# Attention and gated feed-forward on one core: the first quarter of the program put in a written order on all five engines

## The chip, the cores and the metric

The program runs on one core of a Trainium2 chip. The metric is the time of one execution in device microseconds. The core has five engines, each with its own instruction queue that it works off strictly in order: PE (TensorE: matmuls and transposes), ACT (ScalarE), DVE (VectorE), POOL (GpSimd) and SP (SyncE, which here only issues DMA transfers). Engines wait for each other through semaphores. PE writes only to PSUM, on-chip accumulators; POOL works in SBUF, the other on-chip memory.

## The reference

Four sequences of 768 positions and 8 heads of 64 go through local attention with block summaries. The result, heads side by side, is the input of a feed-forward layer with a convolution gate.

```python
# attention, per batch and head; block = 32, window = 16
k_sum = k.reshape(B, H, nb, block, D).max(axis=3)
v_sum = v.reshape(B, H, nb, block, D).mean(axis=3)
scores_l = where(|i - j| < window, q @ k.T / sqrt(D), -1e9)
scores_s = q @ k_sum.T / sqrt(D) + log(block)
a = softmax(concatenate([scores_l, scores_s]))
x = a @ concatenate([v, v_sum])
# feed-forward, per batch; x is [768, 512], d_ff = 1024
h = relu(x @ w_in)
conv = conv_w[0] * h[s-1] + conv_w[1] * h[s] + conv_w[2] * h[s+1]
out = (h * sigmoid(conv)) @ w_out
```

`w_in`, `conv_w` and `w_out` reach the core as 64-bit floats, so the kernel also turns their words into 32-bit numbers.

## The kernel before

**Tiles.** The rows are cut into 8 *chunks* of 384 (two per batch, c = 0 to 7). In a chunk, attention goes by 4 *pairs* of heads; pairs are numbered through, so pair n belongs to chunk n // 4. The feed-forward part of a chunk goes by 8 *units*, one for each 128 of the 1024 hidden columns.

**A pair.** Keys `kw` (a window of 96 and 24 block maxima for each of 6 query blocks), queries `q` and values `va` come by DMA. `qk` (line 256) is 12 small matmuls that use 64 rows of PE each: six for the first head, six for the second, in turn, into two PSUM tiles `pq_0` and `pq_1`. DVE adds the mask (278), ACT takes exponentials with their sums (288), DVE inverts the sums (296, 297), and DVE in chunk 0 or POOL later multiplies (300). `tr` (308) is three transposes for one head into the PSUM tile `pt`, of which there is one; ACT, or DVE for half of chunk 0, copies it to `aT` (313, 315). `av` (329) is 12 matmuls for the pair. ACT rounds the result to `xh` (349), DVE takes the rest `xl` (350).

**A unit.** `f1` (411): 12 matmuls of 384 columns, three (high by high, low by high, high by low) for each of four pieces of the contraction; piece cc needs only pair cc of the chunk. Then relu (429), three taps (432 or 434, and 441 twice), tanh (458), product (459), and high and low part of the result, `ghi` (462, ACT) and `glo` (463, POOL). `f2` (480) multiplies finished gates with `w_out`, three matmuls of 512 columns for each step.

**Weights.** A block of `w_in` or `w_out` (eight each) is loaded, decoded (ACT 93, DVE 100 and 101), rounded to a high part by ACT (124) and a low part by POOL (125).

**What sets the order.** In chunks 0 and 1 the framework's scheduler orders every engine from the order in which the code issues work (`slot`, `slot_t`, `slot_av`, `unit`). It may place single matmuls of `qk`, `f1` and `av` apart, and adds *warm* matmuls on zeros (line 78). From chunk 2 on, PE runs in the order of the code and the others are scheduled. DMAs of inputs are issued by SP in order; each waits until the one eight places before it has landed.

Of the kernel before, what the change touches and what calls it, by code (L numbers as in the profile page):

```python
# [16 lines left out]
P = 128  # L17
# [23 lines left out]
EARLY_IN = 2  # L41

OUT_AT = (6, 7, 8, 9, 10, 10, 11, 12)
WARM = {"start": 10, "pq0": 5, "pq1": 12, "pq2": 3, "pq3": 3, "tr": 2, "av": 3, "unit": 3}
EARLY_AT = 3
ORDERED = 2
NGROUP = NCHUNK * NP * 2
# [3 lines left out]
def attention_ffn(ctx, tc, qT, kT, vT, v4, w_in, cwT, w_out, mask8, ident_in, out):  # L51
# [23 lines left out]
    def warm(where, after=None):  # L75
        def go():
            for i in range(WARM.get(where, 0)):
                nc.tensor.matmul(pw, idle[:, :P], idle, start=True, stop=True)  # L78

        if after is None:  # L80
            go()
        else:
            with tc.issue_after(after):
                go()

    warm("start")


    def decode(out, words, n, name):
        lo_word = words[:, 0 : 2 * n : 2]  # L90
        hi_word = words[:, 1 : 2 * n : 2]
        low = sp.tile([P, DM], U32, tag="wl", name=f"wl_{name}", bufs=1)[:, :n]
        nc.scalar.activation(  # L93
            out.bitcast(F32),
            hi_word.bitcast(F32),
            AF.Prelu,
            scale=2.0**-112,
            alpha=2.0**32,
        )
        nc.vector.tensor_scalar(low, lo_word, 29, None, ALU.logical_shift_right)  # L100
# [4 lines left out]
    def load_in(fc):  # L105
        t = raw_a[:, fc, :] if fc < 6 else raw_b[:, fc - 6, :]
        nc.sync.dma_start(t, w_in[fc].bitcast(U32))
        return t

    def split_in(fc, t):  # L110
        weights(t, flat(win_hi, fc), flat(win_lo, fc), f"i{fc}")

    def load_out(fc):
        t = sp.tile([P, 1024], U32, tag="stage", name=f"wo{fc}", bufs=2)
        nc.sync.dma_start(t, w_out[fc].bitcast(U32))
        return t
# [80 lines left out]

    def prep_pair(c, p):
        b, hf = divmod(c, 2)
        st = state[(c, p)]  # L200
        kw = st["kw"]
        if hf == 0:
            k = st["k"]
            ks = cp.tile([P, NB], F32, tag=f"ks{p}", name=f"ks{c * NP + p}")
            kv = k[:, WIN:KL].rearrange("p (n t) -> p n t", t=BLK)
            nc.vector.tensor_reduce(ks, kv, AX.X, ALU.max)
            state[("ks", b, p)] = ks
        if c == 0:
            (nc.gpsimd if p else nc.vector).tensor_copy(
                kw[:, :, :WK], window(k, 1, list(k.ap[0]), WK)  # L210
            )
        ks = state[("ks", b, p)]
        nc.gpsimd.tensor_copy(
            kw[:, :, WK:NK], ks.unsqueeze(1).to_broadcast([P, CB, NB])
        )

    def vmean_pair(c, p):

        b, hf = divmod(c, 2)
        if hf:  # L220
# [12 lines left out]
        if c == 0:
            nc.gpsimd.tensor_copy(
                st["va"][WK:NK, :, :], vm.unsqueeze(1).to_broadcast([NB, CB, P])
            )
        state[("vm", b, p)] = vm

    def group(j):
        c, r = divmod(j, NP * 2)  # L240
        p, t = divmod(r, 2)
        return c, p, t

    def qk(c, p):


        st = state[(c, p)]
        n = c * NP + p
        pq = [
            ps.tile([P, 512], F32, tag="s", name=f"pq{n}_{h}", bufs=2) for h in range(2)  # L250
        ]
        for blk in range(CB):
            i, half = divmod(blk, 2)
            for h in range(2):
                r = slice(h * QB, (h + 1) * QB)
                last = nc.tensor.matmul(  # L256
# [6 lines left out]
        if c == 0:  # L263
# [428 lines left out]
```

## Time and profile before

| | us |
|---|---|
| three timed runs | 403.81, 403.69, 402.52 |
| median | 403.69 |
| profiled execution, its own time | 404.54 |
| its span, first to last instruction | 402.7 |
| first matmul of chunk 2's units in it, after the start | 129.1 |

The span is one execution under the profiler. In what follows "us 60" is 60 us after its start. Up to us 129.1 chunks 0 and 1 run; chunks 2 to 7 take the rest. A matmul's row gives its whole passage through the engine, and the next one starts before it ends, so costs on PE are read from start to start.

### The profile page before, as it was taken

How to read it: one execution, taken by the hardware profiler on the slowest of the kernel's cores; microseconds unless marked ns; L12 is line 12 of the kernel's file. 1: busy time of each engine (PE TensorE's matmuls, PEld its weight loads, DVE VectorE, ACT ScalarE, POOL GpSimd, SP SyncE). 2: the span in 40 equal slices, each digit the busy share in tenths (PEclk: the TensorE clock that was granted, in tenths of full speed). 3: DMA queues.
4: the chain of work that ended last, by engine and by line, in shares of the span. 5: the costliest groups of instructions: out<-in, count | busy, mean ns of one | idle time of the engine just before them, and what ended most of it. 6: DMA issues, size and time to landing. Idle time of an engine off the chain costs nothing.

```text
span 402.7 us, 8927 instructions
## 1 busy us (share of the span) xinstructions
PE 389.2 (97%) x3164; PEld 322.0 (80%) x3173; DVE 254.3 (63%) x792; ACT 252.3 (63%) x774; POOL 145.6 (36%) x179
## 2 busy tenths in 40 slices
PE   7989799999799999999999999999999999999996
PEld 3546677787588888888888888888888888999884
DVE  4998767787665775678765566466664655656200
ACT  3665788898776776757565777666665644344211
POOL 2336444575753233332432333323333332222200
PEclk9999699999899999999999999999999999999999
DMA  8999494477887495646233244334210000000011
GB/s 276 315 362 236 110 270 137 131 244 212 248 187 239 134 315 143 186 124 212 55 105 101 79 113 114 112 87 121 70 61 28 28 2 26 27 28 26 28 52 52
DMA packets 45357, 54.30 MB, mean 135 GB/s; under 512 B 24641, under 2 KB 33025, under 8 KB 45313
## 3 DMA queue, kind: packets, MB, share of 16 engines
q1 hardware_dynamic: 41568, 47.19, 40.7%
q10 hardware_dynamic: 3744, 6.54, 4.7%
q8 instruction: 25, 0.41, 0.5%
q14 instruction: 20, 0.16, 0.1%
HBM read 45.36 MB, written 6.29 MB: 128 GB/s over the span
## 4 chain that ended last, share of the span: by engine, by line
PE 86%; DMA 9%; ACT 1%; POOL 1%; issue 1%; SPq 0%; DVE 0%; POOLq 0%; ACTq 0%; DVEq 0%
PE f L411 33%; PE f L480 33%; PE pq L256 7%; PE xp L329 6%; PE pt L308 5%; DMA va<-v 4%; DMA raw_b<-w_in 2%; DMA wo<-w_out 1%; PE pw L78 1%; DMA mask<-mask 1%; DMA q<-qT 1%; ACT wu_i L93 1%; POOL wout_lo L125 0%; POOL win_lo L125 0%; PE pv L230 0%
## 5 line engine op out<-in xcount | busy, mean ns | idle before, releaser
L463 POOL TENSOR_TENSOR glo<-t,ghi 128x383 fp32r<-128x383 f32 (+1 forms) x64 | 65.0, 1015 | 99.2 <-ACT ghi L462 89.3
L411 PE MATMUL f<-xh,win_hi 128*128 128x384 f32 (+1 forms) x256 | 93.9, 367 | 0.1
L288 ACT ACTIVATE a<-a,nm 128x120 f32<-128x120 f32 x192 | 75.0, 392 | 22.7 <-DVE nm L278 18.2
L441 DVE SCALAR_TENSOR_TENSOR t<-f,cw,t 128x382 f32<-128x382 f32 (+3 forms) x128 | 78.7, 615 | 15.7 <-ACT t L432 13.6
L411 PE MATMUL f<-xh,win_lo 128*128 128x384 f32 (+1 forms) x256 | 88.3, 345 | 0.0
L411 PE MATMUL f<-xl,win_hi 128*128 128x384 f32 (+1 forms) x256 | 87.7, 343 | 0.0
L480 PE MATMUL f<-wout_lo,ghi 128*128 128x512 f32 x192 | 75.7, 394 | 1.6 <-POOL wout_lo L125 1.6
L480 PE MATMUL f<-wout_hi,ghi 128*128 128x512 f32 x192 | 76.0, 396 | 0.0
L480 PE MATMUL f<-wout_hi,glo 128*128 128x512 f32 x192 | 75.2, 393 | 0.0
L300 POOL TENSOR_TENSOR a<-a,sm 128x360 f32<-128x360 f32 x56 | 43.6, 800 | 81.8 <-DVE sm L297 70.5
L278 DVE CUSTOM_DVE_ANT_0 a<-pq,mask 128x120 f32<-128x120 f32 x192 | 47.8, 276 | 30.6 <-ACT a L288 23.9
L458 ACT ACTIVATE t<-t 128x383 f32<-128x383 f32 (+1 forms) x64 | 33.6, 527 | 47.4 <-DVE t L441 45.0
L459 DVE SCALAR_TENSOR_TENSOR t<-t,f 128x383 f32<-128x383 f32 (+1 forms) x64 | 35.4, 553 | 28.9 <-ACT t L458 28.7
L411 PEld LDWEIGHTS f<-xh,win_hi 128*128 128x128 f32 x256 | 49.0, 191 | 3.1 <-issue 0.9
L411 PEld LDWEIGHTS f<-xl,win_hi 128*128 128x128 f32 x256 | 49.1, 192 | 1.1 <-issue 0.5
L411 PEld LDWEIGHTS f<-xh,win_lo 128*128 128x128 f32 x256 | 48.9, 191 | 1.3 <-issue 1.1
L462 ACT CAST ghi<-t 128x383 fp32r<-128x383 f32 (+1 forms) x64 | 32.9, 514 | 19.0 <-DVE t L459 18.1
L256 PEld LDWEIGHTS pq<-kw,q 64*64 64x64 f32 x768 | 26.9, 135 | 19.9 <-issue 13.2
L480 PEld LDWEIGHTS f<-wout_lo,ghi 128*128 128x128 f32 x192 | 36.1, 188 | 7.8 <-POOL wout_lo L125 1.9
L256 PE MATMUL pq<-kw,q 64*64 64x120 f32 x768 | 38.4, 277 | 4.1 <-DMA q<-qT 2.5
L480 PEld LDWEIGHTS f<-wout_hi,glo 128*128 128x128 f32 x192 | 36.0, 188 | 7.7
L480 PEld LDWEIGHTS f<-wout_hi,ghi 128*128 128x128 f32 x192 | 36.2, 188 | 6.4 <-ACT ob L489 0.3
(56 smaller groups left out, 481.6 us busy)
## 6 DMA issues: line engine op xcount, KB each, us to landing
va<-v SPq DMA_DIRECT2D x32, 288.0 KB
kw<-kT SPq DMA_DIRECT2D x28, 288.0 KB
q<-qT SPq DMA_DIRECT2D x32, 192.0 KB
out_dram<-ob ACTq DMA_DIRECT2D x24, 256.0 KB
kT<-kT SPq DMA_DIRECT2D x12, 392.0 KB
vt<-vT SPq DMA_DIRECT2D x12, 384.0 KB
wo<-w_out SPq DMA_DIRECT2D x8, 512.0 KB
raw_a<-w_in SPq DMA_DIRECT2D x6, 512.0 KB
```

The lines of the kernel that those rows point to most:

```text
L256: last = nc.tensor.matmul(pq[h][half * QB : (half + 1) * QB, i * NK : (i + 1) * NK], st["q"][r, blk * QB : (blk + 1) * QB], st["kw"][r, bl ...
L278: nc.vector.tensor_tensor_reduce(a[:, i, :], pq[h][:, i * NK : (i + 1) * NK], mask[:, edge(hf, i), :], -0.125, 3.0e38, ALU.add, ALU.min, n ...
L288: nc.scalar.activation(a[:, i, :], a[:, i, :], AF.Exp, bias=nm[:, h, i : i + 1], scale=-1.0, accum_out=acc[:, h, i : i + 1],)
L300: (nc.gpsimd if n >= NP else nc.vector).tensor_tensor(a, a, sm[:, h, :].unsqueeze(2).to_broadcast([P, 3, NK]), ALU.mult)
L329: last = nc.tensor.matmul(xp[r, blk * QB : (blk + 1) * QB], va[:NK, blk, r], aT[h][:NK, blk * QB : (blk + 1) * QB], start=True, stop=True,)
L411: last = nc.tensor.matmul(ph[:, :n], w[:, fc, cc, :], x[:, cc, :n], start=(cc == 0 and m == 0), stop=(cc == NCC - 1 and m == 2),)
L441: nc.vector.scalar_tensor_tensor(t[:, i0:i1], h[:, hf + k - 1 + i0 : hf + k - 1 + i1], cw[:, fc, k : k + 1], t[:, i0:i1], ALU.mult, ALU.add,)
L458: nc.scalar.activation(t, t, AF.Tanh, scale=0.5)
L459: nc.vector.scalar_tensor_tensor(t, t, 1.0, h[:, hf : hf + ng], ALU.add, ALU.mult)
L462: nc.scalar.copy(hi, t)
L463: nc.gpsimd.tensor_tensor(gated["lo"][:, fc, d0 : d0 + ng], t, hi.bitcast(F32), ALU.subtract)
L480: nc.tensor.matmul(po, gx[:, fc, ss], w[:, fc, :], start=(fc == 0 and m == 0), stop=(fc == NFC - 1 and m == 2),)
```

## The change

Chunks 0 and 1 and the loads around them become a list of 614 steps, and 10 more of warm matmuls. Each names a piece of work, its indices and, where there is a choice, the engine of a copy (`s` ACT, `v` DVE, `g` POOL). The list is run in order with all five engines in manual order, so that each engine's queue is the list with the other engines' steps left out.

Of the choices: 14 copies that ACT made (6 high parts of weights, `wh`, and 8 of gates, `C`) go to POOL. To DVE go 5 copies `xh`, 4 relus, 1 middle tap, 2 copies `C` and 1 `wh`; of the 25 copies `aT` it has 7 instead of 4, and of the 28 multiplications `n` 9 instead of 8. From chunk 2 on, both transposes of a pair stand in one unit, the first ahead of `qk` and the second behind `av`, where before one stood in each of two units.

```diff
-LOADS = "k0 q0 k1 q1 v0 k2 q2 a0 v1 k3 q3 a1 w0 v2 c a2 w1 v3 a3 w2 w3 w4 w5 w6 w7"
-WARM = {"start": 10, "pq0": 5, "pq1": 12, "pq2": 3, "pq3": 3, "tr": 2, "av": 3, "unit": 3}
+ORDER = """
+k1 k0 w0 q0 q1 k8 k9 ks1 w1 w2 ks0 kc0/g z kc1/g kb0 kb1 q2 wy0 wl0 w3 qk0 wu0 w4 wh0/s m0.0
...
+av4 wo9 M6 m6.0 c5.0/s e6.0 D0.0 tr5.1 f0.2.3 K9 wy10 f0.1.3 m6.1 a8 H0.0 c5.1/s wl10 G0.0
+R0.1/s W12 xh4/s kb8 Z2 f0.3.0 wu10 e6.1 hx4 C0.0/g f0.3.1 xl4 T0.1/s wh10/g M7 r6 R0.2/s
...
+    def run(order):
+        for token in order.split():
+            what, at, eng = re.fullmatch(r"([a-zA-Z]+)([\d.]*)(?:/([svg]))?", token).groups()
+            args = [int(x) for x in at.split(".") if x]
+            steps[what](*args, *([eng] if eng else []))
...
+    with tc.manual_schedule(
+        engines={every.PE, every.Activation, every.DVE, every.Pool, every.SP}
+    ):
+        run(ORDER)
...
-        if together:
-            slot_av(j)
+        if j % 2 == 0:
             slot_t(j)
+        slot(j)
+        slot_av(j)
+        if j % 2 == 0:
+            slot_t(j + 1)
```

In the list `k`, `q`, `t`, `a`, `K`, `w`, `W` are loads by SP; `wy`, `wl`, `wu`, `wh`, `wo` the five steps of a weight block (ACT, DVE, DVE, a copy, POOL; blocks 8 to 15 are `w_out`); `m`, `e`, `r`, `n` mask, exponentials, inversion, multiplication; `c` the copy to `aT`; `f` one piece of `f1`; `R`, `T`, `D`, `H`, `G`, `C`, `O` the steps of a gate; `p` a step of `f2`; `Z` warm matmuls.

On PE, before, pair 6 (`kw_518`) and its surroundings in chunk 1's attention:

```order
L256 MATMUL pq_0_660<-kw_518,q_2_555 64x120 x5
L308 MATMUL pt_597<-ident,a_0_537 120x128 x3
L256 MATMUL pq_0_660<-kw_518,q_2_555 64x120
L411 MATMUL f_0_3_827<-xh_325,win_lo 128x384
L411 MATMUL f_0_3_827<-xh_325,win_hi 128x384
L411 MATMUL f_0_3_827<-xl_326,win_hi 128x384
L411 MATMUL f_0_3_827<-xh_325,win_lo 128x384
L78 LDWEIGHTS idle
L78 MATMUL pw<-idle 128x512
L308 MATMUL pt_636<-ident,a_1_544 120x128 x3
L256 MATMUL pq_1_661<-kw_518,q_2_555 64x120 x6
```

Here one matmul of the first head and the second head's six are set apart from the other five: transposes of pair 5 (`a_0`, `a_1`), a piece of the unit `f_0_3` and a warm matmul run between them.

On PE, now, the same pair 6 (`kw_432`) and what stands ahead of it and behind it:

```order
L386 MATMUL pt_0_684<-ident,a_0_572 120x128 x3
L386 MATMUL pt_1_700<-ident,a_1_585 120x128 x3
L504 MATMUL f_0_0_471<-xh_356,win_hi 128x384
L504 MATMUL f_0_0_471<-xl_357,win_hi 128x384
L504 MATMUL f_0_0_471<-xh_356,win_lo 128x384
L317 MATMUL pq_0_718<-kw_432,q_410 64x120
L317 MATMUL pq_1_719<-kw_432,q_410 64x120
L317 MATMUL pq_0_718<-kw_432,q_410 64x120
L317 MATMUL pq_1_719<-kw_432,q_410 64x120
...
L386 MATMUL pt_0_736<-ident,a_0_657 120x128 x3
```

The twelve matmuls of the two heads stand together and alternate, as they do in all 14 pairs of the list; a piece of `f1` is three matmuls of one unit in a row.

On SP, now, the loads around the third block of `w_out` (`wo_628`, token `W10`):

```order
L155 DMA wo_469<-w_out 128x1024
L155 DMA wo_481<-w_out 128x1024
L242 DMA q_499<-qT 128x384
L257 DMA va_420<-vm_309 24x6x128
L257 DMA va_426<-vm_373 24x6x128
L227 DMA kw_568<-kT 128x6x96
L220 DMA kT_579<-kT 128x784
L220 DMA kT_590<-kT 128x784
L249 DMA va_608<-v 96x768
L155 DMA wo_628<-w_out 128x1024
L242 DMA q_648<-qT 128x384
L227 DMA kw_651<-kT 128x6x96
```

Before, the first block of `w_out` was issued behind the keys of pair 10; now three stand ahead of the queries and keys of pair 8 (`q_648`, `kw_651`).

On ACT, now, the same block's decoding and the first gate (`t_0`):

```order
L522 ACTIVATE f_0_0_471<-f_0_0_471 128x384
L532 ACTIVATE t_0_742<-f_0_0_471,cw 128x383
L144 COPY aT_0_765<-pt_0_736 120x384
L354 ACTIVATE a_0_761,pq_1_719<-a_0_761,nm_759 128x120 x3
L119 ACTIVATE wu_781<-wo_628 128x512
L561 ACTIVATE t_0_742<-t_0_742 128x383
```

The first gate's tanh (line 561) stands behind the decoding of `wo_628`.

## Rows read from the trace of the kernel before

**Rows 1.** The page's first part: busy time, share of the span and instructions of each engine.

```profile
PE 389.2 (97%) x3164; PEld 322.0 (80%) x3173; DVE 254.3 (63%) x792; ACT 252.3 (63%) x774; POOL 145.6 (36%) x179
```

**Rows 2.** Busy time of all engines by stretch: the stretch, its length, then PE, weight loads, DVE, ACT and POOL busy (instructions), granted PE clock as a share, share of the 16 DMA engines, GB/s.

```profile
0.00:34.00 34.00, 29.48 (x281) 16.08 (x286) 26.81 (x90) 18.32 (x68) 11.36 (x20) 1.00 0.99 317
34.00:55.50 21.50, 18.71 (x131) 14.22 (x132) 15.73 (x50) 15.32 (x44) 10.84 (x11) 0.84 0.69 169
55.50:129.10 73.60, 70.99 (x616) 55.32 (x618) 54.59 (x184) 60.31 (x197) 41.15 (x48) 0.98 0.71 202
80.00:100.00 20.00, 20.00 (x173) 16.23 (x174) 16.49 (x52) 17.57 (x55) 12.39 (x15) 1.00 0.70 224
129.10:172.50 43.40, 43.40 (x391) 37.99 (x389) 29.75 (x94) 31.61 (x98) 14.30 (x20) 1.00 0.66 196
172.50:402.70 230.20, 226.58 (x1754) 198.42 (x1751) 127.46 (x376) 126.72 (x371) 67.97 (x82) 1.00 0.24 72
```

**Rows 3.** PE's instructions in order of time: start and length in us, line, operation, tiles, count. First two places in chunk 1, then one pair and a lone transpose row in chunk 2.

```profile
54.32 0.49 PE L308 MATMUL pt<-ident,a 128*120 128x128 f32 x3
54.74 0.83 PE L256 MATMUL pq<-kw,q 64*64 64x120 f32 x12
...
133.49 0.84 PE L256 MATMUL pq<-kw,q 64*64 64x120 f32 x24
134.27 0.92 PE L329 MATMUL xp<-aT,va 120*64 120x64 f32 x24
135.12 0.54 PE L308 MATMUL pt<-ident,a 128*120 128x128 f32 x3
135.41 0.42 PE L411 MATMUL f<-xh,win_hi 128*128 128x384 f32 x1
...
137.59 0.39 PE L480 MATMUL f<-wout_hi,ghi 128*128 128x512 f32 x1
...
139.66 0.49 PE L308 MATMUL pt<-ident,a 128*120 128x128 f32 x3
139.90 0.42 PE L411 MATMUL f<-xh,win_hi 128*128 128x384 f32 x1
140.16 0.34 PE L411 MATMUL f<-xl,win_hi 128*128 128x384 f32 x1
```

**Rows 4.** Busy time of single lines by stretch (columns as above, PE and weight loads alone): line 256 (`qk`), line 411 (`f1`) in two stretches, line 78 (warm matmuls).

```profile
55.50:129.10 73.60, 12.40 (x170) 8.52 (x168) 0.98 0.71 202
...
55.50:129.10 73.60, 35.15 (x144) 24.67 (x144) 0.98 0.71 202
129.10:172.50 43.40, 18.72 (x97) 16.36 (x97) 1.00 0.66 196
...
55.50:129.10 73.60, 3.39 (x11) 1.04 (x14) 0.98 0.71 202
```

**Rows 5.** One of PE's instructions in order of time, with the idle time before it and what ended it.

```profile
106.66 0.56 PE L480 MATMUL f<-wout_lo,ghi 128*128 128x512 f32 x1 [1.64 <-POOL wout_lo L125]
```

**Rows 6.** DMA issues with their sizes (KB each).

```profile
va<-v SPq DMA_DIRECT2D x32, 288.0 KB
kw<-kT SPq DMA_DIRECT2D x28, 288.0 KB
q<-qT SPq DMA_DIRECT2D x32, 192.0 KB
...
kT<-kT SPq DMA_DIRECT2D x12, 392.0 KB
vt<-vT SPq DMA_DIRECT2D x12, 384.0 KB
wo<-w_out SPq DMA_DIRECT2D x8, 512.0 KB
```

**Rows 7.** Groups of instructions by line and shape over the whole span: count, busy us, mean ns of one, idle before.

```profile
L458 ACT ACTIVATE t<-t 128x383 f32<-128x383 f32 x32 | 16.7, 525 | 19.9 <-DVE t L441 19.2 <-DVE sm L297 0.7
...
L434 DVE TENSOR_SCALAR t<-f,cw 128x385 f32<-128x385 f32 x24 | 14.9, 620 | 14.1 <-ACT f L429 11.5 <-POOL glo L463 1.7
...
L206 DVE TENSOR_REDUCE ks<-kT 128x24 f32<-128x768 f32 x12 | 11.4, 947 | 1.4 <-DMA kT<-kT 1.4
...
L300 DVE TENSOR_TENSOR a<-a,sm 128x360 f32<-128x360 f32 x8 | 5.7, 755 | 0.0
...
L93 ACT ACTIVATE wu_o<-wo 128x512 f32<-128x512 f32 x8 | 5.4, 675 | 0.0
...
L313 DVE COPY aT<-pt 120x384 f32<-120x384 f32 x4 | 2.2, 550 | 0.3 <-PE pt L308 0.2
...
L209 POOL COPY kw<-k_xl 128x576 f32<-128x576 f32 x2 | 1.3, 670 | 3.0 <-DMA k_xl<-kT 3.0
```

**Rows 8.** POOL's and DVE's instructions in order of time around us 38: one DVE step of a weight block while POOL works on another, and the same step with no POOL instruction beside its start.

```profile
36.70 3.01 POOL L125 TENSOR_TENSOR win_lo<-wu_i,win_hi 128x512 fp32r<-128x512 f32 x2 [1.99 <-ACT win_hi L124]
...
38.67 1.59 DVE L101 SCALAR_TENSOR_TENSOR wu_i<-wu_i,wl_i 128x512 uint32<-128x512 uint32 x1
...
40.83 0.69 DVE L101 SCALAR_TENSOR_TENSOR wu_i<-wu_i,wl_i 128x512 uint32<-128x512 uint32 x1
```

**Rows 9.** The multiplication of one pair on POOL in chunk 3, and the next pair's `qk` on PE.

```profile
205.69 1.54 POOL L300 TENSOR_TENSOR a<-a,sm 128x360 f32<-128x360 f32 x2 [4.45 <-DVE sm L297]
...
208.70 0.85 PE L256 MATMUL pq<-kw,q 64*64 64x120 f32 x24
```

More of the change, by code (lines that the diff above doesn't have):

```diff
@@ L1 @@
+import re
 import numpy as np
@@ L73, in attention_ffn, with zeros, bits @@
     pw = ps.tile([P, 512], F32, tag="f2", name="pw", bufs=1)
[L75 to L92, printed above, removed]
+    def zeros(n):
+        for _ in range(n):
+            nc.tensor.matmul(pw, idle[:, :P], idle, start=True, stop=True)
+    zeros(10)
+    def bits(out, words):
+        n = words.shape[-1] // 2
         nc.scalar.activation(
             out.bitcast(F32),
-            hi_word.bitcast(F32),
+            words[:, 1 : 2 * n : 2].bitcast(F32),
             AF.Prelu,
@@ L99, in decode, with low_bits, join @@
         )
-        nc.vector.tensor_scalar(low, lo_word, 29, None, ALU.logical_shift_right)
+    def low_bits(words, name):
+        n = words.shape[-1] // 2
+        low = sp.tile([P, DM], U32, tag="wl", name=f"wl_{name}", bufs=1)[:, :n]
+        nc.vector.tensor_scalar(
+            low, words[:, 0 : 2 * n : 2], 29, None, ALU.logical_shift_right
+        )
+        return low
+    def join(out, low):
         nc.vector.scalar_tensor_tensor(
@@ L249, in qk, with first_half, edge @@
+    def first_half(n):
+        return n // NP % 2 == 0
+    def edge(n, i):
+        if first_half(n) and i == 0:
+            return 0
+        if not first_half(n) and i == CB // 2 - 1:
+            return 2
+        return 1
+    def qk(n):
+        st = of(n)
         pq = [
@@ new lines, in masked @@
+    def masked(n, h, i):
+        st = of(n)
+        if i == 0:
+            if h == 0:
+                small(n)
+            st["a", h] = sp.tile([P, 3, NK], F32, tag="a", name=f"a{n}_{h}", bufs=4)
+        nc.vector.tensor_tensor_reduce(
+            st["a", h][:, i, :],
+            st["pq"][h][:, i * NK : (i + 1) * NK],
+            mask[:, edge(n, i), :],
+            -0.125,
+            3.0e38,
+            ALU.add,
+            ALU.min,
+            st["nm"][:, h, i : i + 1],
+        )
@@ L410, in f1 @@
             ):
-                last = nc.tensor.matmul(
+                nc.tensor.matmul(
                     ph[:, :n],
@@ L436, in gate_conv, with taps @@
             )
+        held[c, fc] = h, t
+    def taps(c, fc):
+        hf, n, ng = sizes(c)
+        h, t = held[c, fc]
         for k in (0, 2):
@@ L602, in unit @@
         assert len(pending) <= 2
[L603 to L604 removed]
         for x in pieces[u]:
             f2(*x)
[L607 removed]
+        if c == NCHUNK - 1:
             gates(0)
[L609 to L625 removed]
+    with tc.manual_schedule(engines={every.PE}):
+        for c in range(FIRST, NCHUNK):
+            pieces = work(c)
+            for u in range(NFC):
+                unit(c, u, pieces)
     for pair in ((2, 3), (4, 5)):
```

630 lines of the change are left out of this document (328 added, 302 removed).

## Prediction

> **What bounds the kernel now.** I read the page's busy line first [rows 1]: PE is busy 97% of the span, DVE and ACT 63%, POOL 36%. That says "PE-bound" but is an average over two different programs, so the table of stretches comes next [rows 2]. From us 129.1 on PE is busy 43.40 of 43.40 us and then 226.58 of 230.2, the clock granted at 1.00: nothing but less PE work could shorten that part, and the change leaves its work as it was but for the transposes. So the answer lies before us 129.1, and the question is when the first units of chunk 2 start.
>
> There PE is also "busy" 70.99 of 73.6 us from us 55.5 on, but with much that is no progress. Two views show it. In the order of time [rows 3] the 24 small matmuls of a pair take 0.78 us from start to start in chunk 2 (133.49 to 134.27), both heads passing together; at us 54.74 twelve of them, one head alone, already show 0.83. The busy time by line [rows 4] sums it up: 12.40 us for seven pairs of `qk`, where seven at 0.845 would be 5.9, so 6.5 us are lost to split pairs; 35.15 us for 144 matmuls of `f1` where chunk 2 has 18.72/97 = 0.193 each, 27.8 in all, so 7.4 are lost to small changes of work and to the clock (0.98); and 3.39 us of warm matmuls. Some of it is cheap filling: PE does it while it would wait anyway. Open waits are few; the longest there is 1.64 us, for POOL's low weights at 106.66 [rows 5]. Beside PE, in the same 73.6 us, DVE is busy 54.59 (74%), ACT 60.31 (82%), POOL 41.15 (56%) [rows 2]. So once PE's padding goes, DVE and ACT are close behind.
>
> **The part behind chunk 1.** A transpose row between `f2` and `f1` costs 0.24 (139.66 to 139.90), and the `f1` after it 0.26 instead of some 0.17, so about 0.33 with what it does to its neighbour [rows 3]. In its new place it stands ahead of `qk`: 0.42 from its start to `qk` in the one such place of the trace (54.32 to 54.74), and behind `av` the step to the next work is 0.29 (135.12 to 135.41). One row in each unit becomes two in every other unit; price out and price in differ by hundredths, and over 23 pairs I count some 0.3 us either way, an estimate: zero. What covers the earlier place: POOL's multiplication of a pair ends at 205.69 + 1.54 = 207.23, and `qk` starts at 208.70 [rows 9], 1.5 us of slack. A new wait is possible: the PSUM tile `pt` exists once, so the second transposes wait for the copy of the first, some 0.55 us [rows 7]; `qk` and `av` between them last 0.78 + 0.85 = 1.63 [rows 3]. If ACT were so late that the copy never fitted, PE would wait with all that is queued behind (`f1`, `f2`) up to about 0.5 us a pair, 23 times, 11 us. I take 0, with 11 as the bound on the slow side, none on the fast side since PE has no idle time there to win.
>
> **Chunks 0 and 1: the point I time.** I look for a place in the list with the same PE work behind it as before had at us 55.5, and find it at the first piece of the fourth unit (`f0.3.0`). Behind it stand 156 matmuls of `f1` at 0.182 (135.41 to 137.59 holds twelve, the first of them slow), 28.4 us; 48 of `f2` at 0.23 (nine from 137.59 to 139.66), 11.0; seven `qk` and seven `av` at 0.845 and 0.85 [rows 3, 9], 11.9; 13 transposes at 0.33, 4.3; three small ones, 0.3. That is 56 us, where before took 73.6.
>
> When does it come? `f1` has three PSUM buffers. The fourth unit needs the first gate's last reading, `G0.0`, on DVE, which waits for the tanh `H0.0` on ACT, and ACT's queue has the decoding of `W10` ahead of it, as the order rows of ACT show. A queue in strict order cannot step aside, so all of it waits for a load. Up to and including `W10` SP issues 8 key blocks of 392 KB, 11 weight blocks of 512 (`w_in` blocks have the same size as `w_out`'s), 8 queries of 192, 4 key windows and 7 values of 288, 5 values of 384 [rows 6]: 15,392 KB, 15.8 MB. At the 317 GB/s of the first 34 us that is 50 us; by before's own course, 317 x 34 us + 169 x 21.5 us = 14.4 MB by us 55.5 and then 202 GB/s [rows 2], it is 62. The two ends stay for the range. I take 57, since the list issues loads ahead of need but SP also waits for staging buffers. To it come the decoding 0.68, tanh 0.53 [rows 7], the product, taken as a tap, 0.62 and about 0.5 for signals, so `f0.3.0` at about us 59.5, some 4 us later than the same point of before.
>
> **Chunks 0 and 1: from there to the end.** PE needs 56 us. DVE: before did 54.59 in its stretch. Behind `f0.3.0` the list has fewer block maxima and sums (six fewer at 0.947) and fewer weight steps (five, near 0.69 [rows 8]), together some 9 us less [rows 7]; and more of these: four multiplications at 0.755, four relus, four more taps and two products `G` at 0.62, and nine copies at 0.55 (three `aT`, three `xh`, two `C`, one `wh`) [rows 7], together 3.0 + 6.2 + 5.0, 14 us. That makes about 59. A DVE copy from PSUM or a relu in this shape is not in the trace; between the 0.55 of the copy of 120x384 and the 0.755 of a two-operand step, and I take the nearest. ACT is relieved of 14 copies that went to POOL and 16 steps that went to DVE, near 0.5 each, some 14 us over the whole phase, and falls out of the race. POOL gets 14 copies near 0.67 (measured for 128x576) [rows 7], 9 us over the phase against 63.35 busy of 129.1 (11.36 + 10.84 + 41.15) [rows 2]; it has the room on average.
>
> So PE has 56 us and DVE 59. Neither can run without gaps when five queues wait on each other in strict order. In the densest 20 us of before, 80 to 100, PE was busy 100%, ACT 88%, DVE 82% [rows 2]; in 55.5 to 129.1 DVE had 74%, while PE and not DVE was the bound. I take PE at 90% of useful work and DVE at 94%: 62 and 63 us, and the larger ends the phase at 59.5 + 63 = 122.5, where before had 129.1. The gain is 6.6 us. The profiled execution was 404.54 (span 402.7 and 1.84 around it), the median 403.69, 0.85 lower; so 404.54 - 6.6 - 0.85 = 397.1. I say 397.
>
> **A rule weighed.** Where POOL's and DVE's instructions meet, the trace shows a price: with a low-part subtraction on POOL from 36.70 on (two in 3.01 us), DVE's combining step at 38.67 took 1.59 us, and 0.69 without one beside it at 40.83 [rows 8]. The Trainium skill, SBUF — State Buffer, section "Who interferes with whom", says that the two engines share a pair of ports under an exclusive lock and that whichever started first holds it for its whole instruction, for the forms of DVE instruction it lists; the trace agrees with its 1.59 against 0.69. By that rule the 14 copies on POOL add up to 14 more such chances.
>
> **Rivals.**
> First, slower: DVE becomes the bound, because in a written list a late producer holds all that is behind it. Its price depends on DVE's busy share behind `f0.3.0`. At the 82% of the densest stretch 59 us become 72, the phase ends at 131.5, and the time is 404.54 + 2.4 - 0.85 = 406.1; at the 74% of before it would be 80 and 139, some 414. It decides below 59/69.6 = 85%. For it: 14 us more DVE work, with the added steps small and each between two engines. Against: in before DVE's waits were mostly for work that PE and ACT did late, and a PE with 15 us less padding and an ACT with less to do hand over sooner.
> Second, no change: the loads arrive no earlier than before's did, `W10` at 62 and `f0.3.0` at 64.5; with 63 us behind, the phase ends at 127.5, some 402. For it: 0.69 and 0.71 DMA share [rows 2], so loads are throttled by the order and by staging buffers, not by bytes; and the list loads keys of pairs 8 to 11 before they are needed. With a little more loss it is no change at all, 403.7.
> Third, much faster: loads at 317 GB/s throughout, `f0.3.0` at 53.5, and 59 to 60 us behind it: the phase ends at 113, time 387.6. For it: DMA share 0.99 in the first 34 us shows the rate can be had; against: it was not held for 20 us more.
> Fourth, the meeting of POOL and DVE: 14 copies of 0.67 us, each adding at most the 0.9 us that the trace shows (1.59 - 0.69) to a DVE step, are between 0 and 12.6 us of DVE time; where a third meets one, some 4 us, the phase ends at 126.5 and the time is 401.1. The rule named above stands behind this rival; the rows carry it.
> Fifth, slower: `pt` makes the second transposes wait, up to 11 us, 408; with 1.1 us of slack by the rows I give it little.
>
> **How the numbers follow.** My forecast (phase ends between 118 and 126) has a chance of 0.45; much faster 0.14; the meeting of POOL and DVE as the main loss 0.12; loads no earlier 0.10; DVE's gaps 0.14; `pt` 0.05. About 0.3%, 1.2 us, is what a measurement of this kernel can tell from no change. Forecast, much faster and POOL's meeting all end below that, and of loads no earlier some 4 in 10: faster 0.74. Of the loads half, and of DVE's gaps a quarter, lie within: same 0.08. The rest is slower, 0.18. The range is 387.5 to 406.1: its lower end is the third rival, its upper end the first at 82%. Outside lie the worse half of DVE's gaps and of `pt`, and the best of the third rival.
>
> **What the profile after would show.** The first 128x384 matmul of chunk 2 near us 122.5 (below 118 or above 131 the forecast is wrong). `qk` as whole pairs near 0.85, in the sum of its line about 6 us for seven pairs. `f0.3.0` near us 59.5, with PE's wait ahead of it put down to DVE or ACT; the landing of `W10` near 57. DVE's busy share from there to the end near 94%; at 85% or less the forecast is wrong for its first reason. No idle PE at the second transposes in chunks 2 to 7, and that part as long as before within 1 us; if it is longer, the one-copy `pt` was not covered. DVE's weight steps near 0.7, or 1.5 where a POOL copy stands beside them.

## The result and the profile after

The changed kernel takes 406.01 us (median of 5 runs, 405.59 to 407.81), the kernel before 402.69 us (5 runs, 402.52 to 403.81): a ratio of 1.008, 95% interval 1.0052 to 1.0109. It is slower by 3.3 us where 6 us faster was forecast.

The profiled execution of the changed kernel took 405.67 us with a span of 403.9. That of before took 404.54, which is 1.85 us above the median now known; so the two spans lie 1.2 us apart where the medians lie 3.3 apart, and what follows from the traces is read with that in mind.

The page's busy line and the table of stretches of the changed kernel, at the borders of [rows 1, 2] (columns as there):

```profile
PE 375.4 (93%) x3147; PEld 315.4 (78%) x3147; DVE 262.7 (65%) x809; ACT 244.4 (61%) x744; POOL 152.3 (38%) x192
```

```profile
0.00:34.00 34.00, 23.34 (x187) 11.37 (x188) 25.64 (x71) 18.18 (x57) 16.11 (x22) 0.90 0.99 345
34.00:55.50 21.50, 15.63 (x185) 11.71 (x187) 18.47 (x66) 13.48 (x50) 10.54 (x16) 0.93 0.98 275
55.50:129.10 73.60, 65.39 (x639) 53.56 (x633) 63.60 (x205) 54.00 (x170) 42.55 (x54) 0.97 0.66 196
...
60.83:130.66 69.83, 61.51 (x588) 50.23 (x586) 60.85 (x190) 51.29 (x160) 41.16 (x52) 1.00 0.66 195
...
130.66:403.90 273.24, 269.58 (x2141) 237.85 (x2138) 153.74 (x468) 157.57 (x467) 82.39 (x102) 1.00 0.28 81
```

Chunk 2's first unit starts at us 130.66, not 122.5, and 1.6 us later than before. From there to the end it takes 273.24 us, where before took 402.7 - 129.1 = 273.6: the late part is as good as unchanged. Within the same borders PE is busy less (65.39 us against 70.99 in 73.6), and DVE more (63.60 against 54.59). The fourth unit's first piece, the point that the prediction timed, starts at 60.83.

From there PE now stands and waits. This is the view of what ended PE's idle time from us 60.8 to 130.66 (instruction, what it waited for; us in total, times, longest):

```profile
PE f L504 <- DVE t L566: 5.1, 3, 3.1
PE pv L285 <- DVE sm L365: 1.8, 1, 1.8
PE f L504 <- DMA va<-vm: 0.7, 1, 0.7
PE pq L317 <- DVE sm L365: 0.3, 1, 0.3
PE xp L402 <- DVE xl L434: 0.2, 1, 0.2
```

Nearly all of it is for DVE: the product of a gate (line 566) frees a PSUM buffer of `f1`, and it comes late. Why, DVE's instructions in order of time show (pieces between us 90 and 118; in brackets the idle time before, and what ended it):

```profile
90.86 0.95 DVE L262 TENSOR_REDUCE ks<-kT 128x24 f32<-128x768 f32 x1 [1.02 <-POOL kw L271]
...
99.64 0.95 DVE L262 TENSOR_REDUCE ks<-kT 128x24 f32<-128x768 f32 x1 [1.02 <-POOL kw L271]
...
104.42 0.94 DVE L262 TENSOR_REDUCE ks<-kT 128x24 f32<-128x768 f32 x1
...
108.40 0.55 DVE L566 SCALAR_TENSOR_TENSOR t<-t,f 128x385 f32<-128x385 f32 x1
...
115.77 1.80 DVE L277 TENSOR_REDUCE vs<-vt 128x24 f32<-128x768 f32 x2
...
117.56 0.94 DVE L262 TENSOR_REDUCE ks<-kT 128x24 f32<-128x768 f32 x1
```

These six reductions (four of line 262, two of line 277) are not in the list; the row of line 566 among them is the gate's product that ended PE's longest wait, 3.1 us. They make four block maxima `ks` and two block sums `vs` for pairs 16 to 19, that is chunk 4. Their code stands behind the list and is scheduled, and the scheduler set them between the list's steps, on DVE's queue:

```order
L545 SCALAR_TENSOR_TENSOR t_1_1321<-f_1_1_1203,cw,t_1_1321 128x385
L262 TENSOR_REDUCE ks_2143<-kT_1896 128x24
L545 SCALAR_TENSOR_TENSOR t_1_1321<-f_1_1_1203,cw,t_1_1321 128x384
```

The section on the change above said that each engine's queue is the list with the other engines' steps left out. For DVE, and for SP, which issues the loads of these keys and values among the list's own, that was not so. The two waits of 1.02 us come with it: `ks` of pair 16 takes the buffer of pair 8's, and must wait until POOL has copied it for pair 12. So the foreign steps hold DVE for 6 x 0.94 = 5.6 us of work and 2.0 us of waiting.

### The profile page after: what moved, and what is told of

It reads as the page before. It is cut to its first block, busy times and chain, and to the rows that moved or that the text cites. A ratio compares the mean times of both kernels' runs of the same rounds, so it can differ in the third digit from the quotient of the medians.

```text
span 403.9 us, 8865 instructions
## 1 busy us (share of the span) xinstructions
PE 375.4 (93%) x3147; PEld 315.4 (78%) x3147; DVE 262.7 (65%) x809; ACT 244.4 (61%) x744; POOL 152.3 (38%) x192
## 4 chain that ended last, share of the span: by engine, by line
PE 71%; DVE 15%; ACT 5%; issue 4%; POOL 2%; DMA 1%; SPq 0%; POOLq 0%; ACTq 0%; DVEq 0%
PE f L607 30%; PE f L504 26%; PE xp L402 5%; PE pq L317 5%; PE pt L386 5%; DVE t L545 4%; ACT a L354 3%; DVE a L341 2%; DVE vs L277 2%; DVE wu L136 2%; DMA q<-qT 1%; DVE wl L130 1%; PE pw L112 1%; DVE ks L262 1%; POOL glo L584 1%
## 5 line engine op out<-in xcount | busy, mean ns | idle before, releaser
L584 POOL TENSOR_TENSOR glo<-t,ghi 128x383 fp32r<-128x383 f32 (+1 forms) x64 | 65.6, 1026 | 87.8 <-ACT ghi L144 76.4
L504 PE MATMUL f<-xh,win_hi 128*128 128x384 f32 (+1 forms) x256 | 92.4, 361 | 5.9 <-DVE t L566 5.1
L504 PE MATMUL f<-xl,win_hi 128*128 128x384 f32 (+1 forms) x256 | 86.7, 339 | 0.0
L504 PE MATMUL f<-xh,win_lo 128*128 128x384 f32 (+1 forms) x256 | 86.5, 338 | 0.0
L341 DVE CUSTOM_DVE_ANT_0 a<-pq,mask 128x120 f32<-128x120 f32 x192 | 46.1, 277 | 30.3 <-ACT a L354 25.0
L386 PE MATMUL pt<-ident,a 128*120 128x128 f32 x192 | 33.9, 287 | 6.4 <-DVE aT L146 3.0
L144 ACT CAST ghi<-t 128x383 fp32r<-128x383 f32 (+1 forms) x54 | 27.7, 512 | 19.9 <-DVE t L566 19.9
L144 ACT COPY aT<-pt 120x384 f32<-120x384 f32 x57 | 28.0, 491 | 15.6 <-PE pt L386 15.6
```

The source lines that it names most:

```text
L144: nc.scalar.copy(out, x)
L341: nc.vector.tensor_tensor_reduce(st["a", h][:, i, :], st["pq"][h][:, i * NK : (i + 1) * NK], mask[:, edge(n, i), :], -0.125, 3.0e38, ALU.a ...
L386: nc.tensor.transpose(pt[:NK, i * P : (i + 1) * P], a[:, i, :], ident)
L504: nc.tensor.matmul(ph[:, :n], w[:, fc, cc, :], x[:, cc, :n], start=(cc == 0 and m == 0), stop=(cc == NCC - 1 and m == 2),)
L584: nc.gpsimd.tensor_tensor(gate_at("lo", c, fc), t, hi.bitcast(F32), ALU.subtract)
```

## The experiments

Each run was timed against the kernel before on the same chip; the ratio and its 95% interval are to that kernel, so the changed kernel stands at 1.008. In the traces I read where the fourth unit starts and where chunk 2 starts. There is one profile of each kernel, and these scatter: in runs whose lists are the same up to the fourth unit it starts between us 60.4 and 62.7, and the stretch from there to chunk 2 is 66.6 us in one run and 64.7 in another that only issues two loads later. A difference below 2 us between two traces shows nothing by itself.

**Theory A**: the foreign reductions made the loss. **Rivals**: B, DVE's own added steps in a strict order; C, POOL's copies and their meetings with DVE; D, the transposes of chunks 2 to 7.

### The foreign steps held back (e1_hold)

```diff
+        if (c, fc) == (1, 7):
+            state["last"] = ins.ins
...
                 if first_half(n):
-                    val_sums(n)
+                    with tc.issue_after(state["last"]):
+                        val_sums(n)
...
-                    key_max(n)
+                    with tc.issue_after(state["last"]):
+                        key_max(n)
```

> The six block maxima and sums of pairs 16 to 19, which stand among the list's steps on DVE, are held behind the list's last DVE step (their loads follow them). Theory A, these foreign steps are what lengthens chunks 0 and 1: they hold DVE for 5.7 us of work and 2.0 us of waiting for POOL's copies of block maxima, between us 90 and 118. Chunk 2's first 128x384 matmul then comes at about us 124 to 126 instead of 130.7, and the time falls by 4.5 to 7 us to 399 to 401.5, below the kernel before. Rival B, DVE's own added steps and the strict order set the pace, other gaps open in their place: less than 1.5 us, 404.5 to 406.5. Rival D, the transposes in chunks 2 to 7: no change.

Ratio 1.000 (0.9975 to 1.0025), 402.69 us. Chunk 2 starts at 127.86 instead of 130.66. PE's waits and DVE's busy time in the same stretch:

```profile
PE f L506 <- DVE t L568: 4.4, 6, 1.7
PE pq L317 <- DVE sm L365: 0.3, 1, 0.3
```

```profile
61.28:127.86 66.58, 61.60 (x587) 50.28 (x586) 56.16 (x184) 51.13 (x160) 40.51 (x51) 1.00 0.56 167
```

The edit takes 2.8 us off the phase and, within its interval, undoes the whole slowdown; theory A holds for the sign. The time falls by 3.3 us, between the 4.5 to 7 of theory A and the less than 1.5 of rival B: of the 7.6 us on DVE, less than half was on the path. The loads of these keys and values moved behind the reductions with them (DMA share 0.56 in the stretch against 0.66), so the run doesn't separate the two. The forecast gain is still missing.

### The transposes (e2_one_row_a_unit)

```diff
-        if j % 2 == 0:
-            slot_t(j)
         slot(j)
         slot_av(j)
-        if j % 2 == 0:
-            slot_t(j + 1)
-        elif c == FIRST and u == 0:
-            slot_t(j)
+        slot_t(j)
```

> The list is kept, but from chunk 2 on one transpose row stands in each unit behind av, as in the kernel before. All of the loss is in chunks 0 and 1 (theory A and rival B): 405.5 to 406.5, no change. Rival D, two rows a unit cost PE through the one pt tile or through their neighbours: 2 to 4 us faster, 402 to 404.

Ratio 1.011 (1.0079 to 1.0141). Chunks 2 to 7 take 404.7 - 131.2 = 273.5 us against 273.24: no gain in the old place. Rival D falls.

### The choice of engines

Fourteen copies from POOL back to ACT (e3_copies_on_act), then the thirteen steps that went to DVE back to ACT (e4_dve_to_act), each in the list as it stands (one of the lines touched, for each):

```diff
-wy4 c1.0/v wu2 tr1.1 wl3 t1 wh2/s wu3 wo2 wh3/s w6 w7 wl4 wy5 ks2 wo3 k3 wu4 t8 vs0 wh4/g q5
+wy4 c1.0/v wu2 tr1.1 wl3 t1 wh2/s wu3 wo2 wh3/s w6 w7 wl4 wy5 ks2 wo3 k3 wu4 t8 vs0 wh4/s q5
...
-f0.6.0 e8.1 kb10 av6 wl12 C0.3/v W14 T0.4/s wu12 f0.6.1 a10 wy13 O0.3 D0.4 tr7.0 R0.5/s
+f0.6.0 e8.1 kb10 av6 wl12 C0.3/s W14 T0.4/s wu12 f0.6.1 a10 wy13 O0.3 D0.4 tr7.0 R0.5/s
```

> The 14 copies that the list gives to POOL go back to ACT (6 high parts of weights, 8 of gates). Rival C, POOL's copies lengthen DVE's steps beside them and delay the low parts: 2 to 4 us faster. Theory A and rival B: ACT gets some 7 us more work where it was busy 51 of 70 us, in a strict order; between no change and 3 us slower, 405.5 to 409.

> Of the list's choices for DVE, 4 relus, 1 middle tap, 2 gate copies, 1 weight copy and 5 copies xh go back to ACT (6.6 us less work on DVE, some 6.5 more on ACT); the foreign reductions stay. Rival B, DVE's own added steps are what sets the pace: 3 to 6 us faster, 400 to 403. Theory A: DVE is relieved as well, but its waits for the foreign steps stay and ACT gets the load: 1 us slower to 3 us faster, 403 to 407.

1.0141 (1.0108 to 1.0174) and 1.0159 (1.0122 to 1.0197): both slower than the changed kernel, by some 2.5 and 3 us; the second came out slower than either theory had expected. With the second edit DVE waits more for ACT: 4.7 us before its masks and 2.6 before its taps, where the changed kernel has 3.2 and 0.6. First the view of what ended DVE's idle time with that edit (us 60.77 to 133.85, largest groups), then the changed kernel's:

```profile
DVE a L341 <- ACT a L354: 4.7, 4, 1.5
DVE t L545 <- ACT t L532: 2.6, 3, 1.7
```

```profile
DVE a L341 <- ACT a L354: 3.2, 3, 1.3
DVE ks L262 <- POOL kw L271: 2.0, 2, 1.0
DVE sm L365 <- ACT a L354: 1.1, 2, 0.7
DVE a L341 <- POOL glo L584: 0.9, 1, 0.9
DVE t L545 <- ACT t L532: 0.6, 2, 0.4
```

So the list's choice of engines pays, taken as two groups; single steps were not tried. ACT, busy 51 of 70 us, cannot take these steps back for nothing: DVE waits longer for ACT.

### What one engine's work costs

To weigh the engines, work was taken off one at a time, on top of the first edit, with no change of order: each run leaves out most columns of one kind of step in chunks 0 and 1.

```diff
+            if c < FIRST and k == 2:
+                i1 = i0 + 16
...
+        t = t[:, :16] if c < FIRST else t
         nc.scalar.activation(t, t, AF.Tanh, scale=0.5)
...
+        if eng == "g" and n < 14:
+            a, s = a[:, :, :8], s[:, :, :8]
         by[eng].tensor_tensor(a, a, s, ALU.mult)
```

> On top of e1_hold, the second tap on DVE works on 16 columns in chunks 0 and 1 (its result is left incomplete there), in the same order: 15 or 16 steps of 0.61 us become some 0.1, 8 us less DVE work and 0.5 us less in each gate's chain. If DVE is the bound of chunks 0 and 1 (rival B, with 56.6 us of work in e1_hold's last 67): 5 to 8 us faster than e1_hold's 402.7, 395 to 398. If PE with its changes of work is (61.6 us busy in the same 66.6): at most the 5 us of PE's waits, 398 to 400. If neither: within 1 us.

> On top of e1_hold, the tanh on ACT works on 16 columns in chunks 0 and 1 (result left incomplete there), same order: 16 steps of 0.53 us become some 0.2, 5 us less ACT work and 0.3 us less in each gate's chain. If ACT's place in the chains is what sets the pace (ACT busy 51 of 67 us in e1_hold): 3 to 5 us faster than e1_hold, 398 to 400. If DVE's amount of work sets it: under 1.5 us, 401 to 402.7.

> On top of e1_hold, the 19 multiplications that POOL makes in the list work on 24 of 360 elements each (left incomplete there), same order: some 0.55 us less each, 10 us less POOL work and fewer meetings with DVE's steps. Rival C (POOL's work and its meetings with DVE set the pace): 2 to 5 us faster than e1_hold, 398 to 400.5. DVE or ACT sets it: under 1 us.

| | ratio | interval | fourth unit to chunk 2, us |
|---|---|---|---|
| foreign steps held (e1_hold) | 1.000 | 0.9975 to 1.0025 | 66.6 |
| and 6.1 us less on DVE, 5.3 in the stretch (e6_dve_light) | 0.9924 | 0.9895 to 0.9953 | 62.8 |
| and 5 us less on ACT, 3.8 in the stretch (e7_act_light) | 0.9986 | 0.9967 to 1.0006 | 65.4 |
| and 11 us less on POOL, 4.9 in the stretch (e9_pool_light) | 1.0025 | 1.0002 to 1.0048 | 65.6 |

The shortened steps took 0.234 us on DVE (9.8 us less 3.7, not the 8 us expected), 0.215 on ACT and 0.257 on POOL. DVE's work costs 0.5 us for each us (0.76% of 403 us for 6.1; the intervals allow about half as much more or less), near the exchange of the foreign steps (2.8 to 3.3 us for 7.6). The edit also shortens each gate's chain by 0.38 us; the one on ACT shortens the same chain by 0.31 and gives 0.6 us by its median, not clear of noise, so the chain alone is not what pays. POOL's work costs nothing that can be seen, and the 14 copies brought a loss when they left POOL, so rival C falls for this stretch. Rival B had 5 to 8 us for the DVE edit and got 3. The waits and the stretch with the light DVE show why no more:

```profile
PE f L506 <- DVE t L570: 1.7, 3, 1.1
PE pq L317 <- DVE sm L365: 0.5, 2, 0.3
```

```profile
62.72:125.48 62.76, 60.40 (x588) 50.53 (x586) 50.88 (x186) 51.60 (x162) 41.30 (x51) 1.00 0.59 176
```

PE is now busy 60.40 of 62.76 us. It is the floor here, and DVE's lateness stands on top of it as waits: 61.6 busy and 5.0 idle with the foreign steps held, 61.5 and 8.3 with them.

### The start

The point timed came at us 60.8. Three edits on top of the first ask what holds the start: loads of keys that are needed late (e8_keys_later), a drop of the clock (e10_warm_at_tr), DVE's full queue (e11_early_to_act). In the list, one after the other (of the third, two of its four steps are shown; `c1.0/v` and `kc2/v` change likewise):

```diff
-k1 k0 w0 q0 q1 k8 k9 ks1 w1 w2 ks0 kc0/g z kc1/g kb0 kb1 q2 wy0 wl0 w3 qk0 wu0 w4 wh0/s m0.0
+k1 k0 w0 q0 q1 ks1 w1 w2 ks0 kc0/g z kc1/g kb0 kb1 q2 wy0 wl0 w3 qk0 wu0 w4 wh0/s m0.0
...
-wy4 c1.0/v wu2 tr1.1 wl3 t1 wh2/s wu3 wo2 wh3/s w6 w7 wl4 wy5 ks2 wo3 k3 wu4 t8 vs0 wh4/g q5
+wy4 c1.0/v wu2 tr1.1 wl3 t1 wh2/s wu3 wo2 wh3/s w6 w7 k8 k9 wl4 wy5 ks2 wo3 k3 wu4 t8 vs0 wh4/g q5
...
-wu9 tr4.1 W11 xl3 c4.1/s r5 wh9/s f0.0.3 ks10 n5.0/g qk6 R0.0/s ks11 n5.1/g tr5.0 q10 T0.0/s
+wu9 Z10 tr4.1 W11 xl3 c4.1/s r5 wh9/s f0.0.3 ks10 n5.0/g qk6 R0.0/s ks11 n5.1/g tr5.0 q10 T0.0/s
...
-t0 n0.1/g c0.0/v q3 wh1/s r1 Z2 tr0.1 dcw wo1 c0.1/s q4 wy3 n1.0/v n1.1/v Z4 tr1.0 t2 wl2
+t0 n0.1/g c0.0/s q3 wh1/s r1 Z2 tr0.1 dcw wo1 c0.1/s q4 wy3 n1.0/v n1.1/v Z4 tr1.0 t2 wl2
...
-c1.1/s xl0 pv2 vm1 m2.0 vm2 vc1 a3 e2.0 wl6 Z2 av1 m2.1 q6 wy7 kc3/g e2.1 wu6 a4 xh1/v wh6/g
+c1.1/s xl0 pv2 vm1 m2.0 vm2 vc1 a3 e2.0 wl6 Z2 av1 m2.1 q6 wy7 kc3/g e2.1 wu6 a4 xh1/s wh6/g
```

> On top of e1_hold, the loads of the keys of pairs 8 and 9 (two times 392 KB), issued as the sixth and seventh load, are issued behind the last block of w_in. If the start is held up by loads (the second rival of the prediction): the fourth unit starts 1.5 to 2.5 us earlier than us 61.3 and the time falls by as much, 400.2 to 401.2. If the early stretch hangs on the order of DVE's and ACT's steps and not on loads: within 0.8 us of 402.7.

> On top of e1_hold, ten warm matmuls between the two transposes of pair 4, where PE was idle 2.3 us (us 50.7 to 53.0) and then had a granted clock of 0.50 until about us 59.5. If that drop of the clock costs the start: the clock stays at 1.00 there, the work from us 53 to 59.3 shrinks by up to 3 us, the fourth unit starts at us 58.5 to 60, and the time falls by 1.5 to 3 us against e1_hold (ratio to the kernel before 0.993 to 0.996). If what PE works on there is waited for anyway (DVE and ACT): the fourth unit starts at 60.5 to 61.5 and the ratio stays at 0.999 to 1.002.

> On top of e1_hold, four of DVE's copies before us 36 go to ACT (aT of pairs 0 and 1, first heads; the key window of pair 2; xh of pair 1), 2.7 us less on DVE, which was busy 19.8 of the 20 us from us 20 to 40 while ACT was busy 8.8. If DVE's full queue sets the start: the fourth unit starts some 2 us earlier than 61.3 and the ratio to the kernel before is 0.994 to 0.997. If the chain of attention does: ratio 0.999 to 1.003.

Loads: 0.9997 (0.9971 to 1.0023), the fourth unit at 61.8. Not the loads. The clock: 0.9976 (0.9957 to 0.9994), the fourth unit at 59.0, chunk 2 at 125.3. The fourth unit came where the clock's case had it; the time fell by less than it said (0.993 to 0.996), and beside the 1.000 of the foreign steps held (0.9975 to 1.0025) the gain is not clear of noise. DVE's queue: 0.9990 (0.9965 to 1.0015), the fourth unit at 61.2, although DVE's busy time from us 20 to 40 fell from 19.8 to 17.7: a full queue was not the path.

The clock is read from two stretches (columns as in [rows 2]), the changed kernel first, then the one with ten warm matmuls:

```profile
50.00:53.00 3.00, 0.75 (x13) 0.44 (x9) 1.74 (x13) 2.37 (x10) 0.75 (x2) 0.94 0.99 308
53.00:59.00 6.00, 5.93 (x58) 4.49 (x59) 4.88 (x15) 4.29 (x14) 3.01 (x4) 0.50 0.61 196
```

```profile
50.00:53.00 3.00, 2.78 (x16) 1.38 (x15) 1.92 (x9) 2.36 (x10) 0.31 (x2) 1.00 1.05 306
53.00:59.00 6.00, 4.98 (x66) 3.49 (x65) 5.91 (x23) 5.63 (x17) 3.02 (x4) 1.00 0.93 238
```

PE had stood for 2.3 us between the two transposes of pair 4; then the granted clock was 0.50, its lower level (1.2 GHz), and PE was busy 5.93 of 6 us with 58 matmuls where with the warm ones it did 66 in 4.98. The wait and its price in PE's instructions in order of time, the first two rows from the changed kernel, the third with the warm matmuls:

```profile
53.07 0.90 PE L386 MATMUL pt<-ident,a 128*120 128x128 f32 x3 [2.32 <-DVE aT L146]
55.07 1.48 PE L317 MATMUL pq<-kw,q 64*64 64x120 f32 x24
```

```profile
54.24 0.85 PE L317 MATMUL pq<-kw,q 64*64 64x120 f32 x24
```

The second transposes waited for DVE's copy of the first, because `pt` exists once. This is the fifth rival's mechanism; it showed inside the list and not, as feared, in chunks 2 to 7.

### Together (e12_both, e13_dve_to_pool)

> Both edits of e10 and e11. If each works alone and they add up, the fourth unit starts at 57 to 58.5 and the ratio is 0.988 to 0.993, faster than the kernel before and the changed one; if one of them is hidden by the other, the larger of the two alone; if neither works, 0.999 to 1.003.

> On top of e12_both, seven of DVE's steps in the later part of the list go to POOL (4 multiplications, 2 gate copies, 1 weight copy; 3.2 us less on DVE by e12's own durations, some 5 us more on POOL). e6_dve_light gained 0.4 us for each us taken off DVE, e9_pool_light nothing for 10 us taken off POOL. If that holds where the work is moved and not left out: 1 to 1.5 us faster than e12_both, ratio to the kernel before 0.992 to 0.995. If POOL's longer steps and meetings delay the chains: 0.997 to 1.003.

The seven steps moved to POOL are `n7.0`, `n10.0`, `n12.1`, `n13.0`, `C0.3`, `C1.0` and `wh12`; two of the lines:

```diff
-K11 n7.0/v H0.3 q12 f0.5.2 n7.1/g m8.0 tr6.1 e8.0 G0.3 f0.4.3 wo11 m8.1 f0.5.3 c6.1/s R0.4/v
+K11 n7.0/g H0.3 q12 f0.5.2 n7.1/g m8.0 tr6.1 e8.0 G0.3 f0.4.3 wo11 m8.1 f0.5.3 c6.1/s R0.4/v
...
-f1.2.1 H1.0 c9.0/s R1.1/v e10.0 f1.2.2 G1.0 tr9.1 wh12/v f1.3.0 C1.0/v T1.1/s m10.1 wo12
+f1.2.1 H1.0 c9.0/s R1.1/v e10.0 f1.2.2 G1.0 tr9.1 wh12/g f1.3.0 C1.0/g T1.1/s m10.1 wo12
```

Both start edits: 0.9965 (0.9944 to 0.9986), 400.71 us, about the warm matmuls alone; the fourth unit starts at 60.66, not at 57 to 58.5, so the two don't add up. With seven DVE steps on POOL: 0.9946 (0.9922 to 0.9971), 399.66 us; chunk 2 starts at 126.18, and DVE is busy 54.87 of the 65.67 us from the fourth unit (60.51) on. It is faster than both kernels; that the last edit adds to the one before it (0.8 us by the ratios) is not clear of noise.

## Why the prediction was wrong, point by point

**The sign.** Chunk 2 was to start at 122.5 and started at 130.66, 8.2 us later. The parts: 1.3 us up to the fourth unit (60.8 for 59.5) and 6.8 us behind it (69.8 for 63). By the first experiment 2.8 us of these are the foreign steps with their loads. The other 4 behind the fourth unit come from the two sums and from how they were put together, as follows.

**The step that failed first: DVE's sum.** "Behind `f0.3.0` the list has fewer block maxima and sums (six fewer at 0.947)". The list does; DVE's queue does not, since six of chunk 4's stood in it: nine in the stretch of before, nine now. The sum of 59 us looks good against 60.85 measured only because two errors meet: without the foreign 5.6 the list's own steps come to 55.2. Its multiplications take 0.525 and not 0.755, its copies of gates 0.352 and not 0.55, and four masks, one `xl` and one of the two added products that the sum kept are not in the stretch. These rows of the changed kernel (DVE's groups by line and shape from us 60.8 to 130.7) show both sides:

```profile
L277 DVE TENSOR_REDUCE vs<-vt 128x24 f32<-128x768 f32 x5 | 4.5, 943 | 0.0
...
L262 DVE TENSOR_REDUCE ks<-kT 128x24 f32<-128x768 f32 x4 | 3.8, 947 | 2.0 <-POOL kw L271 2.0
...
L371 DVE TENSOR_TENSOR a<-a,sm 128x360 f32<-128x360 f32 x4 | 2.1, 525 | 0.0
...
L146 DVE CAST ghi<-t 128x383 fp32r<-128x383 f32 x1 | 0.4, 352 | 0.0
```

The order of the changed kernel could have shown it before: four `ks` and five `vs` stand there and the list names three.

**The step that failed second: the larger of two.** "I take PE at 90% of useful work and DVE at 94%: 62 and 63 us, and the larger ends the phase at 59.5 + 63 = 122.5." PE's 62 was 56 us of work and a tenth for gaps. The work alone came to 61.5 us busy, 61.6 with the foreign steps held, and the gaps came on top: PE and DVE wait for each other, so DVE's lateness does not hide under PE's work; it is added as idle time, 8.3 us and, without the foreign steps, still 5.0. The term that was most too small is `f1`: read from start to start, as the sum was, it takes 31.6 us where 28.4 stood, `f2` 12.3 for 11.0, and `qk` with `av` 13.0 for 11.9 (estimates, added up from the rows in order of time). It was priced as in chunk 2, where twelve matmuls stand in a row, and the list takes three at a time. Line 504's busy time, columns as in [rows 4]:

```profile
60.83:130.66 69.83, 35.29 (x157) 1.00 0.66 195
```

That is 0.225 us busy for each, against 0.244 before and 0.193 in chunk 2: less than half of what was to go went. That the short runs are the reason fits the order rows and was not tested.

Without the foreign steps DVE runs at 56.16/66.58 = 84%, not 94. The first rival (DVE's gaps, deciding below 85%) named this; with the foreign steps DVE's share is 87%, and the time came out at what that rival gave, 406.1. That it agrees to 0.1 us is luck, since its share, its start and the foreign steps were not as it said. Its mechanism was the right one in part: the engine that others wait for, not the engine that is full. Lighter DVE work gave 0.5 us for 1.

**Loads and the start.** The chain was seen rightly, its cause was not. SP issued `W10` at us 47.78, and by the table of stretches 345 x 34 us + 275 x 14.8 us = 15.8 MB, as many bytes as were counted, had moved by us 49: the rate of the near end, not of 57. The trace has no landing time for `W10` itself, but ACT's decoding of it stands without idle time behind other work of ACT: the load was not what it waited for. What came late was ACT's queue ahead of it, with pair 6's exponentials. The view of ACT's instructions in order of time, then DVE's product `G0.0` behind them:

```profile
58.76 0.40 ACT L354 ACTIVATE a<-a,nm 128x120 f32<-128x120 f32 x1
59.06 0.15 ACT L354 ACTIVATION_READ_ACCUMULATOR a<-a,nm 128x1 f32 x1
59.12 0.66 ACT L119 ACTIVATE wu<-wo 128x512 f32<-128x512 f32 x1
59.67 0.51 ACT L561 ACTIVATE t<-t 128x383 f32<-128x383 f32 x1
```

```profile
60.22 0.56 DVE L566 SCALAR_TENSOR_TENSOR t<-t,f 128x383 f32<-128x383 f32 x1
```

Decoding and tanh stand side by side as the order said, 0.66 and 0.51 us; both waited for attention, which ran at the lower clock. So 59.5 against 60.83 is a near hit for a wrong reason, and the second and third rival, which both hung on loads, fall: the loads came at the fast rate and nothing followed from it. (The third rival's 53.5 adds 3.5 us to its 50 where the other cases add 2.5; nothing hangs on it.)

**Right.** The transposes: zero forecast, 0.4 us less of span in chunks 2 to 7 (273.24 against 273.6), and the view of PE's waits from us 130.66 on is empty; the one-copy `pt` was covered there. `qk` as whole pairs: 168 matmuls take 7.46 us after the fourth unit's start against 12.40 for 170 in [rows 4] (5.9 forecast). So most of the padding of `qk` went, and of the 11 warm matmuls there two are left, but not that of `f1`; what it gave was eaten by waits and by the later start (60.8 against 55.5).

**POOL and DVE.** The fourth rival's meetings exist. DVE's first step of a weight block took 1.38 and 1.52 us beside POOL's subtractions, and about 0.42 without:

```profile
20.81 3.07 POOL L179 TENSOR_TENSOR win_lo<-wu,win_hi 128x512 fp32r<-128x512 f32 x2 [3.06 <-ACT win_hi L144]
...
25.19 1.26 POOL L179 TENSOR_TENSOR win_lo<-wu,win_hi 128x512 fp32r<-128x512 f32 x1
```

```profile
20.12 0.43 DVE L130 TENSOR_SCALAR wl<-raw_a 128x512 uint32<-128x512 uint32 x1
...
21.38 1.38 DVE L130 TENSOR_SCALAR wl<-raw_a 128x512 uint32<-128x512 uint32 x1
...
25.22 1.52 DVE L130 TENSOR_SCALAR wl<-raw_a 128x512 uint32<-128x512 uint32 x1
```

They lie where 2.7 us less on DVE moved nothing, so they cost little here. The Trainium skill, SBUF — State Buffer, section "Who interferes with whom", says of the forms of DVE instruction that it lists that whichever engine issues first has the shared ports for its whole instruction; the last pair of rows agrees, DVE's step ending at us 26.74, 0.29 behind the subtraction's end at 26.45. Behind the fourth unit they exist too: DVE's two kinds of weight steps take 0.83 and 0.60 us on average there, against 0.69 and 0.42 alone. But they took 0.79 and 0.55 in the stretch of before, and 0.82 and 0.64 with the 14 copies back on ACT, so these copies are not what they meet; as a rival for the time it fell.

**What stays open.** Why the early stretch takes as long as it does: PE is idle there for short waits of many kinds, and only the one at us 50.7 was tried with an effect on the trace. Giving ACT the copy that this wait is for (`c4.0`) was not tried. Whether the order of the list itself could give the 6.6 us is not shown; the best version here gives 2.2 (0.54% of 403). What of the first edit's gain belongs to DVE's steps and what to the loads behind them is open as well.

## What to carry to other kernels

A written order binds only what is written in it: before counting an engine's work in a stretch, read the engine's queue there and look for names that belong to later work. Where two engines hand work to and fro in strict order, the end is the busy time of the one plus its waits for the other, not the larger of two sums; here a microsecond off the late engine was worth 0.4 to 0.5. Price a step as it stands in the new order: `f1` by threes took 0.225 us each and not the 0.193 of long runs. A wait on PE costs itself, and it can also cost the half clock behind it; ten matmuls on zeros in the wait kept the clock up and were worth about 1 us by the ratios, which is not clear of noise.

## What the runs showed that was not expected

An idle time of 2.3 us on PE was followed by more than 6 us at a granted clock of 0.50, while PE was busy throughout. The trace of the kernel before has the same: behind this wait for a load the clock is 0.66 on average from us 40 to 50, which makes the 0.84 in the second row of [rows 2].

```profile
42.34 1.46 PE L256 MATMUL pq<-kw,q 64*64 64x120 f32 x12 [2.54 <-DMA q<-qT]
```

The clock doesn't fall in every execution, and the time goes with it. Of 93 executions of the kernel before that were timed beside the experiments, the 23 with a mean granted clock of 1.00 took 400.4 to 401.2 us, the four with 0.996 took 401.7 to 401.9, the 30 with 0.99 took 402.0 to 402.5, and the 36 with 0.985 to 0.987 took 403.2 to 405.4. No execution of the changed kernel or of its versions had 1.00 (0.975 to 0.996). So the best version's median of 399.66 us lies some 2.6 us below the kernel before at its usual clock, but less than 1 us below it at its best.

Taking 11 us of work off POOL (4.9 of them in the stretch of 66.58 us where it was busy 40.51) gave no gain (1.0025, interval 1.0002 to 1.0048), while 6.1 us off DVE gave 3 us and 5 us off ACT about 0.6 by its median.
